# RWKV-7 followed by a quick-GELU MLP: the layout of the MLP weights in DRAM, and the size of the packets in which they arrive

## Chip, core and metric

The kernel runs on one core of a Trainium2 chip. The metric is the device time in microseconds of one execution. All times below are from five executions of the kernel before, one of which was taken by the hardware profiler.

## The reference

A linear-attention block (RWKV-7) with batch 4, 8 heads, 768 steps and head size 40 feeds an MLP of 3072 tokens, model width 320 and hidden width 2048. Cut to what matters:

```python
for t in range(S):                                   # per batch and head, state is 40 x 40
    y[t] = r[t] @ state
    Sa = state @ a[t]
    state = state * w[t][None, :] - outer(Sa, b[t]) + outer(v[t], k[t])
x = y.transpose(0, 2, 1, 3).reshape(B * S, H * D)    # 3072 x 320
h = x @ w_in                                         # w_in 320 x 2048
out = (h * sigmoid(1.702 * h)) @ w_out               # w_out 2048 x 320
```

The attention inputs come as float32. `w_in` and `w_out` come as float64; the kernel reads them as 64-bit integers and makes float32 of them on the chip.

## The kernel before, in words

**Units.** The 768 steps are cut into 12 chunks of 64. A unit is one chunk of one pair of batches with all 8 heads, so there are 24 units, and the state goes from unit i to unit i + 2. For a unit the kernel takes logarithms and sums of the decay, scales a, k and b by them (L583, L585, L588: `ak` and `b` times the decay), forms small score matrices (`ps_N`, `ps_A`, `ps_RV`), inverts a triangular 64 x 64 matrix per head in five levels (`ps_level`, each with copies by ScalarE and transposes by VectorE: L747, L686), solves with it (`ps_B`, `ps_Q`, `ps_T`, `ps_X`) and reads out (`ps_y`). The result goes through DRAM (`x_dram`, L917) and comes back transposed (`xT_all`, L921). Two units, one chunk, make 256 tokens, for which the MLP runs: `ps_up` (x times `w_in`), the activation (L942) and `ps_down` (times `w_out`), then a store. All matrix work is float32 in 64 x 64 tiles of TensorE. All matmuls and weight loads of TensorE go through one helper and so stand on line 275.

**Order of the work.** The code adds tasks to a plan (class `Plan`), each with a rank, costs per engine, what it reads and what it writes. `Plan.order` plays the tasks through a model of the engines, including a model of how TensorE's instructions are brought in blocks of 256 (`BLOCK`, `FETCH`, `BESIDE`, L65, L123 to L143), and so fixes one order for each engine. The instructions are then issued in that order; nothing is reordered while the kernel runs. All loads and stores are issued from SyncE (SP), onto one DMA queue. At most eight of these DMAs are under way: an issue waits until the DMA issued eight before it has landed, and for the last readers of the buffer that it fills.

**Loads.** A unit loads `time`, `RV`, `logw` and from the fifth unit `wc` with 128 rows each, and `ak`, `b` and `rv` in two halves of 40 rows each (L475, L464). Rows are of 1280 to 4096 bytes.

**Weights.** `w_in` and `w_out` are brought in four pieces each, eight in all (`weight(n, ...)`, L406 to L447, n from 0 to 7). A piece is 128 rows, one for each partition, of 1280 doubles, that is 10240 bytes a row and 1.31 MB a piece. One DMA on SP (L442) brings it to a place for raw doubles: a buffer `extra` with two places "a" and "b", two places in `w_sb` that are not in use yet, and one in `xT_all`; the list is

```python
    raws = ["a", "w4", "w6", "b", "x", "a", "b", "a"]
```

Then ScalarE reads the high words (L422), and VectorE makes the exponent, the fraction and their sum in five passes (L426, L430, L431, L434, L438), the last of which writes the float32 weights to `w_sb`. The ranks of the pieces (`RANKS`, L244) place the first five within the first three units' work. The order of elements within a partition's 10240 bytes is that in which `ps_up` and `ps_down` read them.

On the host, `kernel` (L1009) lays the arrays out; `pieces` (L1059) makes an array of shape (4, 128, 1280) of 64-bit integers from each weight matrix, one piece after the other, a partition's 1280 in a row.

Of the kernel before, what the change touches and what calls it, by code (L numbers as in the profile page):

```python
# [225 lines left out]
def rwkv7_gelu_quick(ctx: ExitStack, tc: tile.TileContext, time_d, v_d, w_d, wc_d, ak_d, b_d, rv_d, w_in, w_out, out):  # L226
    nc = tc.nc
# [2 lines left out]
    C = 64  # L230
    MID = C // 2
    NU = time_d.shape[0]
    PIECE = w_in.shape[2]
    NF = w_in.shape[0] * PIECE // DM
    NM = NF // 2
    NK = DM // 64
# [18 lines left out]
    plan = Plan(dict(logw=3, wc=3, G=1, wch=3, wz=2, time=2, ak=2, b=2, rv=2, FT=3, GT=1, kh=2, bh=2, zr=2, rz=2,  # L255
                     A=1, B=1, RV=2, E0=2, W0=2, P21=2, PT=2, W=2, E=2, ES=2, EX=2, T=2, Tc=1, QT=1, zraw=2, zT=1, M=2, x=1, xT=3, g=4, ob=1), 4)
    tiles, psums, drams = {}, {}, {}

    def single(name, shape):
        return const.tile(shape, FP32, tag=name, name=name)  # L260
# [27 lines left out]
    def act(n):  # L288
        return {"ACT": 210.0 + 0.76 * n}
# [105 lines left out]

    extra = single("extra", [128, 4 * PIECE])
    xT_all = single("xT_all", [128, plan.slots["xT"], 2 * NK * 128])
# [8 lines left out]
    def weight(n, rank, src):  # L406
        at = raws[n]
        def raw():
            if at == "x":
                return xT_all[:, 1:].rearrange("p s n -> p (s n)").bitcast(INT64)  # L410
            tile, k = spots[at]
            return tile[:, k * PIECE:(k + 2) * PIECE].bitcast(INT64)

        scale = lambda: w_sb[:, n * PIECE:(n + 1) * PIECE].bitcast(INT32)

        before = [("weight", m) for m in range(n) if raws[m] == at]
        there = [("weight", m) for m in range(n) if raws[m] in (f"w{n}", f"w{n - 1}")]
        word = lambda dt, w: raw().bitcast(dt).rearrange("p (n two) -> p n two", two=2)[:, :, w]

        def rebased(t):  # L420

            nc.scalar.activation(scale().bitcast(FP32), word(FP32, 1), ACT.Prelu, scale=2.0 ** -112, alpha=2.0 ** 32)  # L422

        def bounded(t):

            nc.vector.tensor_scalar(scale().bitcast(FP32), scale().bitcast(FP32), least, most, ALU.max, ALU.min)  # L426

        def exponent(t):

            nc.vector.tensor_scalar(word(INT32, 1), scale(), 3, -2 ** 23, ALU.logical_shift_left, ALU.bitwise_and)  # L430
            nc.vector.tensor_single_scalar(scale(), scale(), 3, op=ALU.logical_shift_left)  # L431

        def fraction(t):
            nc.vector.scalar_tensor_tensor(word(FP32, 1), in0=word(UINT32, 0), scalar=2.0 ** -52, in1=word(FP32, 1),  # L434
                                           op0=ALU.mult, op1=ALU.mult)

        def joined(t):
            nc.vector.tensor_add(scale().bitcast(FP32), scale().bitcast(FP32), word(FP32, 1))  # L438

        one, two = 170.0 + 0.48 * PIECE, 150.0 + 1.05 * PIECE  # L440
        T = lambda *names: [(name, n) for name in names]
        plan.add(rank, {"SP": 350.0}, lambda t: nc.sync.dma_start(raw(), src), reads=before, writes=T("wt"), size=128 * PIECE * 8)  # L442
        plan.add(rank, act(PIECE), rebased, reads=T("wt") + there, writes=T("rebased"))
        plan.add(rank, {"DVE": one, "sbuf": True}, bounded, reads=T("rebased"), writes=T("bounded"))
        plan.add(rank, {"DVE": 2 * one, "sbuf": True}, exponent, reads=T("bounded"), writes=T("exponent"))
        plan.add(rank, {"DVE": two, "sbuf": True}, fraction, reads=T("exponent"), writes=T("fraction"))
        plan.add(rank, {"DVE": two, "sbuf": True}, joined, reads=T("fraction"), writes=T("weight"))  # L447

    def weights():
        for n in range(len(raws)):  # L450
            weight(n, RANKS[n], w_in[n] if n < NQ else w_out[n - NQ])
# [636 lines left out]
```

## Time and profile before

| | us |
|---|---|
| five executions | 719.08, 721.26, 723.46, 723.84, 726.84 |
| median | 723.46 |
| the profiled execution: its own time | 723.84 |
| its span, from first to last instruction | 722.1 |
| TensorE matmuls busy (PE) | 675.4 (94%) |
| TensorE weight loads busy (PEld, beside PE) | 568.0 (79%) |
| VectorE busy (DVE) | 428.3 (59%) |
| ScalarE busy (ACT) | 356.7 (49%) |
| GpSimd busy (POOL) | 189.2 (26%) |
| DMA queue q1, all loads and stores | 67.03 MB, 30.9% of 16 engines |

A profile has a page with busy times, a picture of the span in 40 slices (each digit is a tenth of busy time, or of the full clock for PEclk), the DMA packets, and a chain: the work that ended last, followed back from the end, at each step to what released it. "Issue" in it is time in which an engine waited for nothing that the profile shows. Queries of the trace give busy times in chosen stretches, the chain piece by piece, and a timeline in which the idle time before an instruction stands in brackets with what ended it. The trace also holds a record of each DMA packet (queue, size, start and duration) and of each step of a semaphore.

### The profile page before, as it was taken

To read this page: it belongs to the slowest core of one execution; us is meant where nothing else is said; L and a number is where in the kernel's file an instruction comes from. 1 tells how busy PE (TensorE), PEld (TensorE's weight loads), DVE (VectorE), ACT (ScalarE), POOL (GpSimd) and SP (SyncE) were. 2 spreads that over 40 slices of the span, in tenths; PEclk is the share of its full clock that TensorE was granted. 3 is DMA by queue.
4 is the path that set the end of the run, shared out by engine and by line. 5 is a ranking of instruction groups with operands and counts; after the bars stand their busy time and mean duration, and the time that the engine had idled before them with its cause. 6 is when DMAs were issued, how large, how long until landed. Compare 5 with 4: busy or idle time off the path is not lost.

```text
span 722.1 us, 43527 instructions
## 1 busy us (share of the span) xinstructions
PE 675.4 (94%) x20256; PEld 568.0 (79%) x20256; DVE 428.3 (59%) x739; ACT 356.7 (49%) x705; POOL 189.2 (26%) x260
## 2 busy tenths in 40 slices
PE   4576896999999999999999999999999999999997
PEld 3565785799788789987788789887889988887564
DVE  6669878856767556666756655755656566431000
ACT  4465645456564554555465455457456446342020
POOL 8004323422331431330340320431530320200000
PEclk9869998999999999999999999999999999999999
DMA  7963441432341441351440341431430230111000
GB/s 218 355 253 103 163 152 59 120 97 72 118 115 45 118 117 44 96 152 31 119 137 22 107 141 31 119 104 55 119 110 27 77 104 5 40 49 31 20 3 20
DMA packets 31861, 69.82 MB, mean 97 GB/s; under 512 B 5056, under 2 KB 14272, under 8 KB 30656
## 3 DMA queue, kind: packets, MB, share of 16 engines
q1 hardware_dynamic: 31680, 67.03, 30.9%
q8 instruction: 159, 2.61, 1.5%
q14 instruction: 22, 0.18, 0.1%
HBM read 59.15 MB, written 7.86 MB: 93 GB/s over the span
## 4 chain that ended last, share of the span: by engine, by line
PE 85%; DVE 5%; ACT 3%; DMA 3%; issue 3%; POOL 1%; SPq 0%; POOLq 0%; DVEq 0%; ACTq 0%
PE ps_down L275 28%; PE ps_up L275 27%; PE ps_level L275 8%; PE ps_y L275 5%; PE ps_B L275 4%; PE ps_X L275 2%; PE ps_Q L275 2%; PE ps_T L275 1%; PE ps_N L275 1%; PE ps_rz L275 1%; PE ps_A L275 1%; PE ps_zT L275 1%; PE ps_RV L275 1%; DMA extra<-in_w_in 1%; PE ps_cum L275 1%
## 5 line engine op out<-in xcount | busy, mean ns | idle before, releaser
L275 PE MATMUL ps_up<-xT_all,w_sb 64*64 64x256 f32 x3840 | 249.7, 378 | 2.1 <-ACT g L942 1.5
L275 PE MATMUL ps_down<-w_sb,g 64*64 64x320 f32 x3072 | 246.0, 434 | 3.5 <-DVE w_sb L438 2.5
L275 PEld LDWEIGHTS ps_up<-xT_all,w_sb 64*64 64x64 f32 x3840 | 161.4, 133 | 25.8 <-ACT g L942 1.8
L275 PEld LDWEIGHTS ps_down<-w_sb,g 64*64 64x64 f32 x3072 | 135.7, 134 | 48.3 <-issue 5.1
L670 ACT ACTIVATE EX<-ES,quads 128x256 f32<-128x256 f32 x116 | 52.6, 501 | 49.7 <-DVE ES L665 49.5
L591 POOL TENSOR_TENSOR kh<-time,G 128x320 f32<-128x320 f32 x24 | 21.4, 894 | 185.0 <-PE ps_y L275 89.2
L942 ACT ACTIVATE g<-ps_up 128x1024 f32<-128x1024 f32 x48 | 49.1, 1022 | 39.7 <-PE ps_up L275 39.5
L275 PEld LDWEIGHTS ps_level<-W,EX 64*64 64x64 f32 x2560 | 56.5, 134 | 8.8 <-ACT EX L670 1.7
L716 DVE TENSOR_TENSOR E<-two,ps_level 128x256 f32<-128x256 f32 x80 | 33.2, 415 | 40.5 <-ACT W L714 39.7
L275 PE MATMUL ps_level<-W,EX 64*64 64x64 f32 (+1 forms) x2560 | 55.3, 218 | 1.1 <-POOL EX L672 0.6
L714 ACT COPY W<-ps_level 128x512 f32<-128x512 f32 x51 | 29.9, 585 | 42.8 <-PE ps_level L275 42.6
L275 PE MATMUL ps_level<-PT,EX 64*64 64x64 f32 (+2 forms) x1280 | 35.2, 244 | 13.0 <-DVE EX L686 7.3
L968 DVE TENSOR_TENSOR ob<-ob,ps_down 128x320 f32<-128x320 f32 x24 | 11.6, 485 | 59.2 <-ACT ob L966 58.8
L275 PEld LDWEIGHTS ps_level<-PT,EX 64*64 64x64 f32 x1280 | 32.7, 145 | 17.0 <-issue 7.1
L907 POOL TENSOR_TENSOR x<-zr,FT 128x128 f32<-128x128 f32 x84 | 43.4, 546 | 10.0 <-DVE EX L686 9.8
L583 POOL TENSOR_TENSOR ak<-ak,FT 128x512 f32<-128x512 f32 x21 | 28.1, 1340 | 54.9 <-DMA ak<-in_ak 27.5
L845 ACT COPY B<-ps_B 128x416 f32<-128x416 f32 x36 | 18.2, 506 | 43.4 <-PE ps_B L275 43.1
L275 PE MATMUL ps_y<-RV,kh 64*64 64x104 f32 x768 | 36.1, 250 | 2.2 <-DVE M L861 2.2
L275 PE MATMUL ps_y<-M,bh 64*64 64x104 f32 x768 | 36.4, 249 | 1.8 <-issue 1.8
L665 DVE STREAM_TRANSPOSE ES<-E 128x256 f32<-128x256 f32 x80 | 35.6, 445 | 3.9
L861 DVE TENSOR_TENSOR M<-ps_X,later 128x832 f32<-128x832 f32 x24 | 24.5, 1021 | 18.8 <-PE ps_X L275 18.8
L275 PEld LDWEIGHTS ps_y<-RV,kh 64*64 64x64 f32 x768 | 29.9, 133 | 5.6 <-DVE M L861 2.4
(140 smaller groups left out, 1130.6 us busy)
## 6 DMA issues: line engine op xcount, KB each, us to landing
ak<-in_ak SPq DMA_DIRECT2D x48, 160.0 KB
time<-in_time SPq DMA_DIRECT2D x24, 320.0 KB
rv<-in_rv SPq DMA_DIRECT2D x48, 160.0 KB
xT_all<-x_dram SPq DMA_DIRECT2D x48, 160.0 KB
wc<-in_wc SPq DMA_DIRECT2D x20, 264.0 KB
logw<-in_w SPq DMA_DIRECT2D x24, 160.0 KB
b<-in_b SPq DMA_DIRECT2D x48, 80.0 KB
RV<-in_v SPq DMA_DIRECT2D x24, 160.0 KB
```

Source lines behind the costliest of these rows:

```text
L275: nc.tensor.matmul(o, lhsT, rhs, start=start, stop=True, skip_group_check=True)
L583: plan.add(R, {"DVE": 690.0, "POOL": 1270.0, "sbuf": True}, lambda t: of(t.engine).tensor_mul(ahT(), ahT(), FT_of(i)), reads=T("ak", "FT") ...
L591: plan.add(R + 4, {"POOL": 870.0, "DVE": 490.0, "sbuf": True}, lambda t, n=n, dst=dst: of(t.engine).tensor_mul(dst(i)[:, :, :D], by_head(t ...
L665: plan.add(rank, dve(256), lambda t: nc.vector.transpose(ES(n), source(t)), writes=[key("ES", n, 6)], **reads)
L670: nc.scalar.activation(dst[:, :, h], ES(n), ACT.Copy, scale=quads[:, h, :1])
L714: plan.add(rank, any2(512), lambda t: copy(t.engine)(tiles_of(W(n + 1)), blocks(psum(t, ""), 64)), writes=[key("W", n + 1, 5)], pair=pair)
L716: plan.add(rank, dve(256), lambda t: nc.vector.tensor_sub(tiles_of(E(n + 1)), every(two32, [128, 2, 4, 32]), blocks(psum(t, ""), 64)[:, :, ...
L845: plan.add(R, any2(416), lambda t: copy(t.engine)(dst(), psum(t, "")[:, :, :208]), writes=[("Bv", i)] if x and c > 0 else T("B"), pair=(na ...
L861: plan.add(R + 1, dve(832), lambda t: nc.vector.tensor_tensor(M_of(i).rearrange("p (j b) n -> p b j n", b=2), psum(t, "")[:, :, :416].rear ...
L907: of(t.engine).tensor_mul(x[:, b ^ u, b], both(i)[:, at, :64], FT_of(i)[:, at])
L942: plan.add(-45, act(1024), lambda t: nc.scalar.activation(g_of(c * NQ + q).rearrange("p m r n -> p r m n"), psum(t, "").rearrange("p r (m ...
L968: plan.add(-45, dve(320), lambda t: nc.vector.tensor_add(ob_of(serial), ob_of(serial), psum(t, "")[:, 1, :DM]), reads=[("ob", serial)], wr ...
```

## The change

The host lays each piece out as five blocks of 256 doubles for all 128 partitions, one block after the other: shape (4, 5, 128, 256) in place of (4, 128, 1280). A partition's 10240 bytes of a piece so lie in five runs of 2048 bytes, 262144 bytes apart. The DMA that brings a piece reads the five runs of each partition and puts them side by side in the same place as before. What lies in SBUF afterwards, the plan's costs and ranks, and all other instructions are as before: the order of the instructions on the five engines, and what each waits for, is the same in both programs.

```diff
@@ rwkv7_gelu_quick
-    PIECE = w_in.shape[2]
+    PIECE = w_in.shape[1] * w_in.shape[3]
@@ weight
-        plan.add(rank, {"SP": 350.0}, lambda t: nc.sync.dma_start(raw(), src), reads=before, writes=T("wt"), size=128 * PIECE * 8)
+        plan.add(rank, {"SP": 350.0}, lambda t: nc.sync.dma_start(
+            raw().rearrange("p (g n) -> p g n", g=src.shape[0]), src.rearrange("g p n -> p g n")), reads=before, writes=T("wt"), size=128 * PIECE * 8)
@@ pieces, on the host
         x = x.reshape(4, -1, *x.shape[1:]).transpose(0, 2, 1, 3)
-        return np.ascontiguousarray(x.reshape(4, 128, 1280)).view(np.int64)
+        x = x.reshape(4, 128, 5, -1).transpose(0, 2, 1, 3)
+        return np.ascontiguousarray(x).view(np.int64)
```

## The prediction

> **What bounds the kernel now.** I read the page's top first (busy shares, the slices, the packet counts), then the busy table of the stretch in which weights arrive, then the chain of work there and TensorE's own waits, and last the trace's records of single DMA packets and of semaphores.
>
> The page: TensorE is busy almost without a gap from the ninth slice on; its holes, and the only low digits of its clock, lie in the first fifth, where the DMA row is full.
>
> ```profile
> PE   4576896999999999999999999999999999999997
> ...
> PEclk9869998999999999999999999999999999999999
> DMA  7963441432341441351440341431430230111000
> ...
> DMA packets 31861, 69.82 MB, mean 97 GB/s; under 512 B 5056, under 2 KB 14272, under 8 KB 30656
> ...
> q8 instruction: 159, 2.61, 1.5%
> ```
>
> 31861 - 30656 = 1205 packets are of 8 KB or more. 1024 of these are the weights (8 pieces x 128 rows of 10240 B). The 159 of q8 hold 16384 B each, 256 instructions of 64 B: 159 x 256 = 40704, against the 40512 instructions of PE and PEld. So q8 brings TensorE its own instructions, one block of 256 at a time, on the same 16 DMA engines.
>
> The busy table by stretch (columns: time, PE, PEld, DVE, ACT, POOL, granted clock, DMA share, GB/s):
>
> ```profile
> 13.00:24.80 11.80, 7.84 (x319) 6.41 (x312) 9.12 (x14) 5.27 (x14) 4.14 (x4) 1.00 0.98 353
> 24.80:28.30 3.50, 0.05 (x5) 0.04 (x4) 0.95 (x2) 1.86 (x10) 0.20 (x1) 0.70 0.98 311
> 28.30:36.40 8.10, 6.34 (x168) 5.62 (x171) 6.39 (x8) 2.86 (x4) 1.13 (x1) 0.71 1.00 332
> 36.40:50.00 13.60, 9.87 (x271) 9.21 (x265) 9.43 (x13) 8.93 (x17) 0.14 (x1) 0.50 0.86 312
> 130.00:722.00 592.00, 582.25 (x17276) 487.28 (x17268) 326.73 (x607) 286.26 (x556) 145.90 (x182) 1.00 0.27 78
> ```
>
> From 13 to 50 us the DMA engines are full, and in 24.8 to 28.3 no compute engine is. After 130 us TensorE is 98% busy: a lead won early is kept, as its order of work is fixed. The chain of work and TensorE's timeline (in brackets: idle before, and what ended it) say what that hole is:
>
> ```profile
> 14.29 8.55 DMA extra<-in_w_in
> 22.84 0.02 issue
> 22.86 1.42 ACT w_sb L422
> ...
> 24.80 3.45 issue
> 28.26 1.70 PE ps_level L275 x32
> ...
> 34.28 1.31 issue
> 35.59 0.71 PE ps_level L275 x22
> ```
>
> ```profile
> 21.48 0.34 PE L275 MATMUL ps_A<-ak 64*64 64x64 f32 x6 [1.67 <-issue]
> 28.26 1.08 PE L275 MATMUL ps_level<-PT,EX 64*64 64x96 f32 x20 [3.45 <-issue]
> 35.59 0.37 PE L275 MATMUL ps_level<-PT,EX 64*64 64x32 f32 x12 [1.31 <-issue]
> 52.64 0.25 PE L275 MATMUL ps_y<-M,bh 64*64 64x104 f32 x1 [0.77 <-issue]
> ```
>
> "Issue" means no wait that the profile shows. The packet records name it: q8's packets end at 20.10, 26.98, 34.30 and 51.32 us, and TensorE starts again 1.38, 1.28, 1.29 and 1.32 us later. These are waits for instructions. A block is asked for when TensorE enters the block before it, so its wait can be read: packet start less that entry. Packets of q1 that passed on one engine meanwhile are counted beside it.
>
> | fetch asked at, us | DMA traffic | waited, us | packets passed |
> |---|---|---|---|
> | 15.33, 21.48, 28.26, 35.58, 48.42, 79.91 | 55 to 85% weights | 3.70, 4.37, 4.86, 2.81, 1.91, 3.54 | 19.2, 13.6, 22.2, 20.6, 7.6, 11.9 |
> | 195.9, 208.0, 464.8, 514.3 | small packets, 89 to 96% busy | 1.53, 2.58, 1.62, 1.26 | 13.3, 14.8, 15.9, 12.9 |
> | 75 fetches | under 10% busy | mean 0.56 | 0 |
>
> The second row holds the four longest of the twelve fetches past 100 us with over 80% busy; all twelve waited 1.05 us on average. The count that passes is alike (means 15.9 and 14.2), the time is not. A fetch seems to stand behind some 15 packets, whatever their size.
>
> **The change, part by part.** No instruction moves on any engine, and the waits of all five stand as before; only the eight weight DMAs differ, 640 runs of 2048 B for 128 of 10240 B.
>
> *Packets.* The count grows by 8 x 512 = 4096. A 10240-B packet took 388 ns (median of 1024), a 2048-B packet 84 ns (median of 3840). One engine's share of a piece goes from 8 x 388 = 3.10 to 40 x 84 = 3.36 us: +0.26 us a piece. Ends: 40 x 81 (the shortest record) = 3.24 against the old mean 8 x 444 = 3.55 gives -0.3; the mean rate of 1280-B packets (78.6 ns, 61 ns per KB) makes 126 ns of 2048 B, 5.03 us, +1.5. I take +0.26, from rows of just this size. Nearly all of it is covered. By the semaphore records the pieces landed at 22.84, 26.78, 31.14, 37.89, 43.79, 51.93, 84.11 and 110.86 us; ScalarE's L422 read them at 22.86, 32.43, 37.73, 44.76, 57.41, 60.62, 91.38 and 112.40. Only the first has no slack: 0.25 us on the path.
>
> *Issue on SP.* A weight DMA held SP's queue 0.33 to 0.39 us. No DMA with five runs in a row of the tile is in the trace: 0.33 as now, or 5 x 0.33 = 1.7 us. I take 0.33, since rows of 40 and of 128 runs cost the same. Behind it on SP wait the next loads, but in this stretch a DMA lands 4.7 to 14.5 us after its issue, behind others; that backlog covers either end. Without it, 1.3 us for each of eight.
>
> *Fetches.* With 2048-B packets, 15.9 x 84 = 1.3 us; the four small-packet fetches waited 1.75 on average. I take 1.7; ends 0.6 (idle DMA) and 4.9 (no change). Add 1.1 us for the packet and 1.3 to the restart: 4.1 us from asking to running, where three of these took 6.2, 6.8 and 7.3.
> - Fetch of 15.33: there at 19.4, TensorE ran dry at 19.81. Its 1.67 us go, but ScalarE stands behind the first piece until 22.84, so nothing is won on the path.
> - Fetch of 21.48, now asked at 19.8: there at 23.9, needed at about 25.05 (24.80 + 0.25). The 3.45 go whole.
> - Half clock follows that hole: the 1.70 at 28.26 would be 0.87 + 0.43 = 1.3, as the same two groups took at 22.56 and 23.23: 0.4.
> - Fetch of 28.26: asked at 25.05, there at 29.2, needed 5 to 6 us after asking. The 1.31 go.
> - Fetch of 48.42: TensorE used its block in 3.45 us; 0.6 to 1.2 + 1.0 + 1.3 makes 2.9 to 3.5. Of 0.77 I take 0.65.
> - Fetch of 79.91: wait 3.54 to 1.7; its stall of 0.42 at 85.38 goes.
>
> *What is late next.* Led by 5 us, unit 2's ak meets its landing: 34.76 + 3 x 0.26 = 35.5, then POOL's 1.27, against ps_N at 43.49 - 5 = 38.5: enough, but not for much over 6. The sixth piece lands near 53.4 and is wanted at 60.62 - 5.5 = 55.1: enough.
>
> Sum: +0.25 - 3.45 - 0.4 - 1.31 - 0.65 - 0.42 = -6.0 us. The profiled execution took 723.84 us (span 722.1): 717.8. It stands 0.4 above the median of five, so I say 717.5.
>
> **Two rules weighed.** The Trainium skill's "DMA: Bandwidth & Descriptors", section "Queues, rings and completion order", has each DMA engine drain a whole packet of some 9 to 17 descriptors, at most 64, from one ring before it turns to another. This trace's 13 to 22 records fit; 17 x 84 gives 1.4 us and the sum above, but a turn as long as a DMA's 40 runs on one engine would be 3.4 us and leave the stalls as they are. The same page's "Latency and other measured facts" speaks against the change: rows 512 KiB apart in DRAM moved at 207 GB/s. A partition's runs will lie 256 KiB apart; by an estimate from that page a piece would take 1.31 MB / 207 GB/s = 6.3 us. No row here shows it.
>
> **Rivals.**
> 1. *Fetches wait by bytes or by whole DMAs, not by packets.* For: the long waits are also those with the longest backlog in bytes. Against: 89 to 96% busy small-packet stretches let a fetch in after 1.3 to 2.6 us. Then only the 0.25 us stays: 724.
> 2. *The clock stays up too.* It was 0.50 from 36.4 to 50, after holes of 1.31 and 3.04 us. With the first gone, the 9.3 us of TensorE work on the chain between 40.7 and 51 could take about 5 (ps_X 0.94 for 1.66, ps_Q 0.45 for 0.80). The landings above, and the 3.04-us hole, which waits for ScalarE and stays, leave some 3 us of it: 714.5.
> 3. *Slower: the pieces come too slowly.* The first six are one queue, so each one's delay adds up. The sixth is read at 60.62; for +7.2 us it must land at 67.8, 15.9 late, 2.65 a piece: 6.2 us a piece, or 155 ns a packet. Below that the lead is only eaten. For: stretched records exist (a mean of 126 ns at the 1280-B rate, a longest of 595). Against: the median of 84. At 160 ns: 732.
>
> **How the numbers follow.** Main case 0.50 (714.5 to 721, 717.5 likeliest), rival 1 0.25 (722 to 727), rival 2 0.15 (712 to 716), rival 3 0.10 (over 728). The range 713.5 to 726.5 leaves out rival 3 and the outer ends of 1 and 2. About 1%, 7.2 us, is what a measurement tells from no change. Below 716.2 lie rival 2 and a third of the main case: faster 0.30; slower 0.10; within 0.60.
>
> **What would show it.** Right: 35957 packets; no PE idle of over 1 us to "issue" before 60 us; q8 waits near 1.7 us in 13 to 50; ps_level x32 of 28.26 by 25.5; first L422 near 23.1. Wrong: the 3.45 still there (rival 1); 2048-B packets well over 84 ns and L422 waiting at the fourth to sixth piece (rival 3); a clock of 1.00 in 36 to 50 (rival 2); or a lead at 60 us that is gone by 130, where DVE is 85% busy and could give it back.

## The result, and the profile after

| | before | after |
|---|---|---|
| median, us | 723.46 (89 executions, 717.85 to 728.82) | 726.68 (47 executions, 720.89 to 731.23) |
| ratio, 95% interval | | 1.0047 (1.0035 to 1.0059) |
| the profiled execution, us (span) | 723.84 (722.1) | 724.83 (723.0) |
| DMA packets | 31861 | 35957 |

The changed kernel is 3.2 us slower; the interval of the ratio makes it 2.5 to 4.3. The forecast of 717.5 us is missed by 9 us. The direction is that of rival 1, the size more than the rival's 0.25 us.

The page of the kernel after, the same rows as before:

```profile
PE   4676897999999999999999999999999999999997
...
PEclk9759998999999999999999999999999999999999
DMA  7973542332341331351350351431340230111000
...
DMA packets 35957, 69.82 MB, mean 97 GB/s; under 512 B 5056, under 2 KB 14272, under 8 KB 35776
...
q8 instruction: 159, 2.61, 1.5%
```

The change does what it says: 4096 packets more, none of over 8 KB among the weights, the same bytes. TensorE is again busy from the ninth slice on. Its busy table by stretch, with the columns as before:

```profile
13.00:24.80 11.80, 7.44 (x231) 6.85 (x228) 6.55 (x10) 2.95 (x11) 4.47 (x5) 0.86 0.99 336
24.80:28.30 3.50, 3.50 (x108) 3.50 (x99) 2.63 (x4) 2.32 (x3) 0.00 (x0) 0.54 1.03 323
28.30:36.40 8.10, 3.72 (x132) 2.99 (x128) 5.78 (x8) 4.67 (x13) 0.81 (x2) 0.92 1.02 332
36.40:50.00 13.60, 9.47 (x243) 8.79 (x247) 9.10 (x14) 8.01 (x15) 1.18 (x1) 0.50 0.91 308
130.00:722.00 592.00, 582.53 (x17324) 476.98 (x17312) 329.00 (x611) 286.98 (x557) 146.18 (x182) 1.00 0.27 78
```

In the first stretch TensorE runs 231 matmuls where it ran 319: its first hole, which ended at 21.48 us, now ends at 24.24, and what that held up runs in the second stretch, at a clock of 0.54. The second hole has moved behind it, to 28.46. After 130 us TensorE's matmuls are busy as before (582.53 us, 582.25 before). The rate of the loads is the same within 5% in all four early stretches. TensorE's timeline and ScalarE's show the holes (in brackets: idle before, and what ended it):

```profile
24.24 0.34 PE L275 MATMUL ps_A<-ak 64*64 64x64 f32 x6 [2.31 <-issue]
30.31 0.64 PE L275 MATMUL ps_level<-PT,EX 64*64 64x96 f32 x20 [1.85 <-issue]
37.10 0.63 PE L275 MATMUL ps_level<-PT,EX 64*64 64x32 f32 x13 [1.33 <-issue]
```

```profile
25.14 0.37 ACT L657 COPY P<-ps_N 128x256 f32<-128x256 f32 x1 [2.87 <-PE ps_N L275]
25.41 1.39 ACT L422 ACTIVATE w_sb<-extra 128x1280 f32<-128x1280 f32 x1
```

All three holes are there, 2.31, 1.85 and 1.33 us for 1.67, 3.45 and 1.31. The first is now itself on the chain of work, which before passed it by and went through the first piece's landing:

```profile
21.93 2.31 issue
24.24 0.34 PE ps_A L275 x4
```

ScalarE's L422 is late by it too: the first piece landed at 23.02, but its L422 ran at 25.41 (22.86 before), because ScalarE first copies `P` from `ps_N`, and `ps_N` stood behind the hole.

The table of fetches, made from the packet records as in the prediction (asked when TensorE enters the block before; packets of q1 that passed on one engine):

| kernel | asked at, us | waited, us | packets passed |
|---|---|---|---|
| before | 15.33, 21.48, 28.26, 35.58 | 3.70, 4.37, 4.86, 2.81 | 19, 14, 22, 21 |
| after | 15.67, 24.24, 30.31, 37.10 | 6.19, 3.73, 4.28, 3.26 | 67, 35, 38, 39 |

The forecast had 1.7 us. The four waits are 4.37 us in the mean, 3.94 before, and 1.7 to 3.5 times as many packets pass in them.

### The profile page after: what moved, and what is told of

Same layout as the page of the kernel before. It is cut to its first block, busy times and chain, and to the rows that moved or that the text cites. A ratio compares the mean times of both kernels' runs of the same rounds, so it can differ in the third digit from the quotient of the medians.

```text
span 723.0 us, 43527 instructions
## 1 busy us (share of the span) xinstructions
PE 676.6 (94%) x20256; PEld 560.2 (77%) x20256; DVE 428.5 (59%) x739; ACT 356.8 (49%) x705; POOL 190.6 (26%) x260
## 2 busy tenths in 40 slices
DMA packets 35957, 69.82 MB, mean 97 GB/s; under 512 B 5056, under 2 KB 14272, under 8 KB 35776
## 3 DMA queue, kind: packets, MB, share of 16 engines
q8 instruction: 159, 2.61, 1.5%
## 4 chain that ended last, share of the span: by engine, by line
PE 83%; DVE 6%; DMA 3%; ACT 3%; issue 3%; POOL 1%; SPq 1%; POOLq 0%; DVEq 0%; ACTq 0%
PE ps_down L275 28%; PE ps_up L275 26%; PE ps_level L275 8%; PE ps_y L275 4%; PE ps_B L275 4%; PE ps_X L275 2%; DMA ak<-in_ak 2%; PE ps_Q L275 2%; PE ps_T L275 1%; PE ps_rz L275 1%; PE ps_N L275 1%; PE ps_A L275 1%; PE ps_RV L275 1%; PE ps_zT L275 1%; DMA rv<-in_rv 1%
## 5 line engine op out<-in xcount | busy, mean ns | idle before, releaser
L275 PE MATMUL ps_up<-xT_all,w_sb 64*64 64x256 f32 x3840 | 247.0, 378 | 2.8 <-ACT g L943 1.5
L275 PE MATMUL ps_down<-w_sb,g 64*64 64x320 f32 x3072 | 243.2, 434 | 3.3 <-DVE w_sb L438 2.6
L275 PEld LDWEIGHTS ps_up<-xT_all,w_sb 64*64 64x64 f32 x3840 | 157.4, 133 | 28.3 <-ACT g L943 1.8
L275 PEld LDWEIGHTS ps_down<-w_sb,g 64*64 64x64 f32 x3072 | 129.1, 134 | 52.1 <-issue 4.4
L758 ACT COPY Tc<-ps_level 64x128 f32<-64x128 f32 x80 | 20.7, 259 | 26.6 <-PE ps_level L275 25.7
```

The source lines that it names most:

```text
L275: nc.tensor.matmul(o, lhsT, rhs, start=start, stop=True, skip_group_check=True)
L758: copy(t.engine)(at(Tc_t, i)[HALF[r], 128 * h:128 * h + 128], psum(t, "")[HALF[h], r, :128])
```

## The experiments

In the expectations "turn" and "line" are two forms of rival 1: a block of instructions waits for one whole DMA's share of an engine, or for all that stands in the engine in front of it. "Place" is the pitch of 256 KiB in DRAM. All eight pieces are changed unless it is said otherwise. Ratios are to the kernel before on the same chip, with 95% intervals; the kernel before took 725.87 us beside runs10_1k, pad_2k, split5_2k and split4_10k, 725.13 beside stride4_10k, split10_1k, last4_2k and pool_queue, 724.93 beside only_first_2k, first_10k, after_beside and split5_rows, and 722.42 beside paced_10k, split2_rows and before_again. "Mean wait" is that of the second to fourth fetch (asked at about 21 to 39 us) in the one profiled execution, 4.01 us before and 3.76 after.

### Size of packets, one DMA a piece

**runs10_1k**: the changed kernel with ten runs of 1024 B.

```diff
-        x = x.reshape(4, 128, 5, -1).transpose(0, 2, 1, 3)
+        x = x.reshape(4, 128, 10, -1).transpose(0, 2, 1, 3)
```

> Ten runs of 1024 B for each partition in place of five of 2048 B. If the loss of the change comes from each packet's own cost or from SP held up by many descriptors: +3.2 us for 32 more packets an engine and piece, so 72 more give +7, near 730.5 us. If it comes from what stands in line in front of the instruction blocks: 80 packets of about 45 ns make 3.6 us for 3.36, waits grow by 0.3 us each, 727 to 728 us.

Measured: 729.72 us, 1.0056 (1.0027 to 1.0085). Mean wait 3.80 us; 52 to 64 packets passed. A 1024-B packet took 48 ns (median). So packets of 10240, 2048 and 1024 B let a fetch in after about the same time, with 19, 37 and 58 packets in front of it. It is not a count.

**pad_2k**: the changed kernel with 264 doubles (2112 B) from one run of a partition to the next in place of 262144 B, so that the pitch is no power of two.

```diff
+        x = np.pad(x.reshape(4, 128, 5, 256), ((0, 0), (0, 0), (0, 0), (0, 8)))
...
+            raw().rearrange("p (g n) -> p g n", g=5), src[:, :, :256]), ...
```

> Packets of 2048 B with one DMA a piece as changed, but in DRAM a partition's five runs lie close together, 2112 B apart (a pad of 64 B), in place of 262144 B. Theory 'place': near 723.5 us as before. Theories 'turn' and 'line': as changed, 726 to 727.5 us, waits of 3.3 to 6 us.

Measured: 728.3 us, 1.0029 (1.0003 to 1.0055). Mean wait 3.93 us. Without the pitch a loss remains, of 0.2 to 4 us by this interval, and a 2048-B packet takes 84 ns (median) in both kernels. So the pitch is not needed for the loss; that it has no part in it is not shown.

### Number of DMAs a piece

**split5_2k**: the changed layout, five DMAs of 128 x 2048 B for one.

```diff
-            raw().rearrange("p (g n) -> p g n", g=src.shape[0]), src.rearrange("g p n -> p g n")), ...
+        ... lambda t: [nc.sync.dma_start(raw()[:, 256 * g:256 * g + 256], src[g]) for g in range(5)], ...
```

> The changed layout, but each piece is brought by five DMAs of 128 x 2048 B in place of one DMA with 640 runs; packets stay at 2048 B, one engine's share of a DMA falls from 40 packets (3.36 us) to 8 (0.67 us). Theory 'turn' (an instruction block waits until the DMA in progress has ended on its engine): waits of the blocks asked for in 13 to 50 us fall from 3.3 to 6.2 us to 1.5 us or less, the holes by issue go, and the time is near 717 us. Theory 'line' (it waits for the time of all that stands handed over on its engine, whatever the DMA): eight DMAs under way hold less, but the line is still some microseconds: waits 2 to 4 us, 721 to 725 us. Theory 'place' (runs 256 KiB apart in DRAM are slow): near 726.7 as changed.

Measured: 723.07 us, 0.9957 (0.9935 to 0.9979). Mean wait 2.61 us. It is faster than both kernels.

**split10_1k**: the same with ten DMAs of 1024-B runs.

> Ten DMAs a piece, each of 128 runs of 1024 B; one engine's share of a DMA is 8 x 48 ns = 0.38 us, and SP needs about 10 x 0.33 = 3.3 us to issue a piece, about what it takes to move. Theory 'line': with at most eight DMAs under way the line is at most 3 us and mostly half of it: waits of 1 to 2.5 us, holes of 2 us or less in all before 60 us, ratio 0.990 to 0.996. Against it, SP's issue time may hold the pieces back: the first would land by 1 us later, and then the ratio is 0.996 to 1.002.

Measured: 724.11 us, 0.9993 (0.9970 to 1.0015). Mean wait 1.23 us. Its timeline shows no idle time of TensorE put down to "issue" between 12 and 95 us: what the forecast wanted of the change is here, and nothing is won. (The profiled execution took 727.73 us, 3.6 more than the median of this kernel.) The stretch from 13 to 50 us of this kernel, then of the kernel before:

```profile
13.00:50.00 37.00, 24.23 (x746) 21.58 (x742) 25.74 (x34) 19.08 (x43) 5.75 (x6) 0.71 0.80 240
```

```profile
13.00:50.00 37.00, 24.10 (x746) 21.28 (x742) 25.89 (x35) 18.92 (x43) 5.61 (x6) 0.72 0.94 329
```

The same 746 matmuls in the same time, but the loads move at 240 GB/s for 329. GpSimd's timeline and TensorE's in this kernel name the new wait:

```profile
41.92 1.41 POOL L584 TENSOR_TENSOR ak<-ak,FT 128x512 f32<-128x512 f32 x1 [15.01 <-DMA ak<-in_ak]
```

```profile
33.59 1.56 PE L275 MATMUL ps_level<-PT,EX 64*64 64x96 f32 x32 [2.78 <-DVE EX L687]
40.53 1.56 PE L275 MATMUL ps_level<-PT,EX 64*64 64x96 f32 x32 [4.95 <-DVE EX L687]
```

SP spends some 0.4 us on each of ten issues, and unit 2's `ak`, two DMAs, is issued behind them by 36.7 us (27.1 before) and lands at 41.4; GpSimd takes it up at 41.92. Before, the same step was

```profile
35.27 1.27 POOL L583 TENSOR_TENSOR ak<-ak,FT 128x512 f32<-128x512 f32 x1 [8.79 <-DVE extra L434]
```

In split10_1k VectorE's and TensorE's work waits behind this step.

**split4_10k** and **stride4_10k**: the kernel before with four DMAs of 32 rows of 10240 B, neighbouring rows in the one, every fourth row in the other.

```diff
-lambda t: nc.sync.dma_start(raw(), src)
+lambda t: [nc.sync.dma_start(raw()[32 * g:32 * g + 32], src[32 * g:32 * g + 32]) for g in range(4)]
...
+lambda t: [nc.sync.dma_start(raw()[g::4], src[g::4]) for g in range(4)]
```

> The layout before (packets of 10240 B), but each piece is brought by four DMAs of 32 rows: one engine's share of a DMA falls from 8 packets (3.10 us) to 2 (0.78 us). Theory 'turn': waits of 1.5 us or less, near 717 us, the same as with five DMAs of small packets, since packet size does not matter. Theory 'line': the same as there too, 721 to 725 us. If packet size matters once the DMA is small: this one is slower than the five DMAs of 2048-B packets by over 2 us.

> As the four DMAs of 10240-B packets before, but each takes every fourth row, so that it spreads over all partitions (the 32 neighbouring rows of the last try took 774 ns a packet for 388, which spoiled it). One engine's share of a DMA is 2 packets, 0.78 us, near that of the five DMAs of 2048-B packets (0.67). Theory 'line', in time of what stands ahead, whatever its packets: waits of 1.6 to 3.9 us in 13 to 50 as with those five, and 721 to 725 us where before takes 725.9 (ratio 0.994 to 0.998). If packets of 10240 B hold a block up more than those of 2048 at the same size of DMA: no gain over before, waits of 2.8 to 4.9.

Measured: split4_10k 744.16 us, 1.0255 (1.0215 to 1.0295). It can't be compared on the fetches (10.26 us for the first, 1.59 in the mean of the next three), since its 10240-B packets took 774 ns for 388 (medians): 32 neighbouring rows arrive at half the rate. stride4_10k 724.5 us, 0.9995 (0.9973 to 1.0016), mean wait 2.03 us. Its shorter waits bought nothing, since ScalarE's first L422 ran at 31.46 us:

```profile
31.46 1.35 ACT L422 ACTIVATE w_sb<-extra 128x1280 f32<-128x1280 f32 x1 [7.25 <-DMA b<-in_b]
```

The first piece had landed by 22.68. But in this kernel ScalarE's waits ahead of that L422 are for the semaphores of the first three pieces' DMAs (in split5_2k for those of the first piece alone), and the last DMA of the third landed at 31.31. So the run says nothing on what shorter waits are worth.

### Which pieces, and which queue

**last4_2k**: 2048-B runs in one DMA for `w_out`'s four pieces alone. **only_first_2k**: for the first piece alone. **first_10k**: for all but the first. **after_beside**: the changed kernel again, beside the last two. The edit picks the old or the new `dma_start` (and the layout to go with it) by n; for first_10k:

```diff
+        ... nc.sync.dma_start(raw(), src...) if n == 0 else nc.sync.dma_start(
             raw().rearrange("p (g n) -> p g n", g=src.shape[0]), src.rearrange("g p n -> p g n")), ...
```

> Only the four pieces of w_out (the fifth to the eighth) come in packets of 2048 B; the four of w_in come as before. If the change's loss of 0.47% arises in 13 to 40 us, where the first four pieces and the three holes lie: ratio 0.999 to 1.002. If it arises later, or piece by piece: 1.002 to 1.005.

> Of the eight weight pieces only the first comes as 640 runs of 2048 B in one DMA; the other seven come as 128 rows of 10240 B, as in the kernel before. What is open is where the changed kernel's 3.2 us (ratio 1.0047) are made. 'First': at the first piece, where the fetch asked at 15.67 waited 6.19 us (3.70 before), so that TensorE was late for ps_N and ScalarE's first L422 ran at 25.41 in place of 22.86. Then this kernel loses nearly all of it: a first fetch of about 6 us, first L422 at 25 or later, ratio 1.003 to 1.005. 'Every': each of the eight adds its 0.26 us or holds SP up a little. Then one piece of eight is worth 0.4 us: ratio 1.0005, first L422 near 23.1.

> The complement: the first piece comes as 128 rows of 10240 B, the other seven as 640 runs of 2048 B each in one DMA. 'First': the loss is gone, ratio 0.998 to 1.001, first L422 near 22.9, later fetches still waiting 3 to 5 us as in both kernels. 'Every': seven eighths of the loss stay, ratio 1.004.

> The changed kernel itself, unaltered, beside the three others. By its 47 earlier runs: ratio 1.0047 (1.0035 to 1.0059) of the kernel before; the first fetch wait, 6.19 us in its one profiled execution, should again be over 5 us by 'first'. If it comes out near 3.7 with the same loss, the first piece is not where the time is lost.

Measured: last4_2k 726.7 us, 1.0018 (0.9995 to 1.0041); only_first_2k 724.86, 1.0003 (0.9981 to 1.0026); first_10k 726.38, 1.0027 (1.0000 to 1.0054); after_beside 727.46, 1.0035 (1.0007 to 1.0062). In only_first_2k the first fetch did wait 6.47 us and the first L422 ran late:

```profile
25.44 0.37 ACT L658 COPY P<-ps_N 128x256 f32<-128x256 f32 x1 [4.68 <-PE ps_N L275]
25.71 1.40 ACT L422 ACTIVATE w_sb<-extra 128x1280 f32<-128x1280 f32 x1
```

Yet its time hardly moved: "first" had 1.003 or more, and the interval ends at 1.0026. In first_10k, with L422 at 22.64, the ratio is still 1.0027, though its interval reaches down to 1.0000. "First" falls; the intervals of these runs hold what "every" says, but are too wide to show it.

**pool_queue**: the kernel before with the weights issued by GpSimd, on a queue of their own.

```diff
-lambda t: nc.sync.dma_start(raw(), src)
+lambda t: nc.gpsimd.dma_start(raw(), src)
```

> Packets of 10240 B and one DMA a piece as before, but the eight weight DMAs are issued from GpSimd, on a queue of their own; the first five are free to go at about 11 us, so the DMA engines are as full from 11 to 45 us. If the line in which an instruction block waits is that of the DMA engine, over all queues: waits of 3 to 5 us between 13 and 45 us, as before. If each queue has its own line and the engine takes turns between queues: loads and blocks go beside the weights, waits of 1 to 2 us. The time says little, since the pieces compete with the first units' loads from 11 us on: 715 to 735 us.

Measured: 725.15 us, 0.9993 (0.9967 to 1.0019). The first four fetches waited 5.69, 4.00, 4.08 and 1.17 us, the last of them when 0.83 MB stood queued, the others at 2.8 MB and more. A queue of their own for the weights did not shorten the waits.

### Shorter DMAs, or a slower issue

**split5_rows**: the kernel before, its own layout, five DMAs of 2048 B of each row. **paced_10k**: 1276 of a row's 1280 doubles in one DMA and the last four in four DMAs of 8 B a row. **split2_rows**: two DMAs of 5120 B of each row.

```diff
-lambda t: nc.sync.dma_start(raw(), src)
+lambda t: [nc.sync.dma_start(raw()[:, 256 * g:256 * g + 256], src[:, 256 * g:256 * g + 256]) for g in range(5)]
...
+lambda t: [nc.sync.dma_start(raw()[:, at:to], src[:, at:to]) for at, to in [(0, 1276), (1276, 1277), ..., (1279, 1280)]]
...
+lambda t: [nc.sync.dma_start(raw()[:, 640 * g:640 * g + 640], src[:, 640 * g:640 * g + 640]) for g in range(2)]
```

> The kernel before with its own layout in DRAM, but each piece fetched by five DMAs of 256 doubles of each row, that is 2048-B packets whose runs lie 10240 B apart. It asks whether the gain of the five DMAs (ratio 0.9957 with the blocked layout) needs the new layout. 'Line' (an instruction block waits for whole DMAs' shares of an engine, so shorter DMAs shorten it, wherever they lie in DRAM): the same gain, ratio 0.994 to 0.998, fetch waits of 1.6 to 3.9 us in 13 to 50 us. 'Place' (contiguous blocks matter): packets longer than 84 ns in the median and no gain, ratio 1.000 or more.

> The kernel before, where each piece's DMA brings 1276 of a row's 1280 doubles (one run of 10208 B) and four more DMAs bring the last four, 8 B a row each. SP is so held for five issues a piece, as in split5_rows, but 99.7% of a piece stay in one DMA. 'Line' by the size of single DMAs: fetch waits of 13 to 50 us stay at 3 to 6 us, ratio 1.000 to 1.004. 'Pace' (five issues spread the backlog in the engines, and that alone shortens the waits): waits of 1.6 to 3.4 us as in split5_rows, ratio 0.993 to 0.998.

> The kernel before with each piece fetched by two DMAs of 640 doubles of each row, 5120-B packets. 'Line' by the size of single DMAs: waits between those of one DMA (2.8 to 4.9 us in 13 to 40 us) and of five (1.6 to 2.9): 2.2 to 3.5, ratio 0.997. 'Pace': two issues are 1 us of SP, so little is spread: ratio 0.998 to 1.000.

Measured: split5_rows 720.7 us, 0.9950 (0.9921 to 0.9980); paced_10k 719.92, 0.9968 (0.9944 to 0.9993); split2_rows 722.15, 0.9996 (0.9968 to 1.0025). Mean waits 2.43, 1.85 and 2.50 us. split2_rows has waits as "line" had them and a time as "pace" had it: its waits are as short as those of the kernels with five DMAs, and nothing is won. So a shorter mean wait alone, read in one profile, does not make the gain. The gain needs neither the new layout nor small packets: paced_10k brings 99.7% of a piece in rows of 10208 B by one DMA. "Pace" holds, and "line" by the size of single DMAs falls. SP's timeline shows the pace, in paced_10k some 3.5 to 4.8 us for the issues of a piece (first fence) where a piece's one issue took 0.33 before (second fence):

```profile
13.08 3.50 SPq L442 DMA_DIRECT2D extra<-in_w_in  x5
17.45 4.78 SPq L442 DMA_DIRECT2D w_sb<-in_w_in  x5
23.09 4.43 SPq L442 DMA_DIRECT2D w_sb<-in_w_in  x5
```

```profile
14.29 0.33 SPq L442 DMA_DIRECT2D extra<-in_w_in  x1
```

Two things make this pace, and no run separates them. One is SP's own time, 0.34 us an issue in the mean before and 0.44 to 0.57 in the three kernels with five DMAs a piece (first six pieces). The other is the program's rule of at most eight DMAs under way, of which one piece now takes five. Of the 4.78 us of the second piece, 2.70 pass until the first piece lands at 21.41 and makes room; in split5_rows 20 of the first 30 weight issues start within 0.06 us of such a landing, in paced_10k 6.

TensorE's timeline in paced_10k:

```profile
21.62 0.34 PE L275 MATMUL ps_A<-ak 64*64 64x64 f32 x6 [2.15 <-issue]
26.20 0.64 PE L275 MATMUL ps_level<-PT,EX 64*64 64x96 f32 x20 [1.26 <-issue]
45.59 0.48 PE L275 MATMUL ps_B<-RV,A 64*64 64x104 f32 x9 [1.53 <-issue]
49.32 0.30 PE L275 MATMUL ps_y<-M,bh 64*64 64x104 f32 x1 [1.10 <-issue]
```

The 3.45-us hole of before is one of 1.26, the 1.31 at 35.59 is gone, and new ones come at 45.59 and 49.32.

What a slower issue changes can be counted: the backlog, the bytes of all DMAs issued by SP when a fetch is asked for, less the bytes that the packet records show as moved by then. Means of the second to fourth fetch:

| kernel (packets of weights) | backlog, MB | wait, us |
|---|---|---|
| before, before_again (10240 B) | 2.67, 2.18 | 4.01, 3.33 |
| after, after_beside (2048 B) | 2.07, 2.12 | 3.76, 4.14 |
| runs10_1k (1024 B) | 1.70 | 3.80 |
| split2_rows (5120 B) | 1.80 | 2.50 |
| split5_2k, split5_rows (2048 B) | 1.06, 1.12 | 2.61, 2.43 |
| stride4_10k (10240 B) | 1.07 | 2.03 |
| paced_10k (10208 B) | 0.76 | 1.85 |
| split10_1k (1024 B) | 0.36 | 1.23 |

Over these and the four other kernels with all issues on SP (split4_10k with its slow packets left out; only_first_2k, first_10k, last4_2k, pad_2k: 2.09 to 2.44 MB, 3.22 to 3.93 us) the correlation of the two columns is 0.88. Sorted by size of packet they show nothing: 1024 B has both 3.80 and 1.23 us.

The backlog is not the whole of it. By single fetches, not means of three, the correlation is 0.72. And the first fetch, which the table leaves out, goes the other way: it waited 6.19 and 6.12 us in the two profiles of the changed kernel with 1.68 and 1.90 MB queued, 4.75 in before_again with 2.95. During the 6.19 us the queue of loads moved 2.14 MB, more than had stood there, so bytes issued after the fetch was asked for went ahead of it. The second to fourth fetch of before let only 1.2 to 1.6 of 2.4 to 3.0 MB pass. So a fetch neither waits for all that is queued nor for that alone; what decides between it and the loads stays open.

### The spread of single profiles

**before_again**: the kernel before, unaltered, one execution with a profile.

> The kernel before, unaltered, for a second profile. If its first fetch, asked at about 15.3, again waits 3.4 to 4.2 us, the 6.1 to 6.5 us of the kernels whose first piece comes in 2048-B packets are an effect of the change; if it waits 5 us or more, that wait varies between executions by more than the change moves it, and no single profile can carry the 3 us.

Measured: 723.03 us. Its first fetch waited 4.75 us (3.70 in the other profile), and its holes differ as well:

```profile
22.69 0.34 PE L275 MATMUL ps_A<-ak 64*64 64x64 f32 x6 [2.98 <-issue]
29.74 1.07 PE L275 MATMUL ps_level<-PT,EX 64*64 64x96 f32 x20 [3.72 <-issue]
52.09 0.25 PE L275 MATMUL ps_y<-M,bh 64*64 64x104 f32 x1 [1.65 <-issue]
```

It falls between the two cases that were set out. The start of one and the same matmul, later or earlier than in the first profile of before (us):

| at, in before | before_again | after | after_beside | only_first_2k | split5_rows | paced_10k |
|---|---|---|---|---|---|---|
| 21.60 | +1.21 | +2.76 | +2.38 | +2.56 | -0.43 | +0.13 |
| 41.40 | +0.37 | +1.97 | +3.94 | +1.49 | -4.02 | -3.64 |
| 50.91 | -1.44 | +2.11 | +1.64 | +0.68 | -6.15 | -3.66 |
| 59.23 | -0.76 | +1.16 | +1.62 | +0.80 | -2.15 | -2.03 |
| 73.86 | +2.17 | +1.17 | +4.58 | +3.67 | -3.01 | -2.02 |
| 716.90 | -0.89 | +0.90 | +2.85 | +0.73 | -5.16 | -1.21 |

Two executions of the same program differ by 1 to 2 us at such points. That is the size of what is looked for, and only medians of many executions carry it. Nor is a profiled execution a typical one: it took 722.62 us in paced_10k (median 719.92) and 717.30 in split2_rows (median 722.15).

## Why the prediction was wrong, point by point

- **Packets: right.** 35957 packets; a 2048-B packet took 84 ns in the median. The pieces landed at 23.02, 27.33, 32.23, 38.59, 44.09 and 52.58 us, 0.2 to 1.1 later than before.
- **Issue on SP: right in what the others felt, not in what SP did.** A weight's issue held SP 0.38 us, but some 0.8, and one issue behind them 3.09:

```profile
13.59 0.81 SPq L442 DMA_DIRECT2D extra<-in_w_in  x1
...
18.23 0.39 SPq L442 DMA_DIRECT2D w_sb<-in_w_in  x1
18.67 3.09 SPq L465 DMA_DIRECT2D wc<-in_wc  x1
```

  The backlog covered it as said: unit 2's `ak` was issued at 23.10, 22.91 before.
- **Fetches: this step failed.** The prediction had "A fetch seems to stand behind some 15 packets, whatever their size". It rested on the likeness of two means, 15.9 packets among weights and 14.2 in stretches of small packets. With 2048-B packets the second to fourth fetch let 34.7 to 38.9 pass, with 1024-B packets 51.8 to 63.6, and waited as long as before. What goes with the wait is the backlog in bytes, which the change leaves much as it is (2.07 and 2.12 MB for 2.67 and 2.18): eight pieces of 1.31 MB put into the engines by issues of 0.3 to 0.4 us. The small-packet stretches had short waits with DMA engines as busy, but the forecast did not ask how much stood queued there. It was 0.40 to 0.60 MB at the four fetches in the second row of the prediction's table, and 0.83 to 3.00 MB at the six in the first row, so what was held against rival 1 agrees with it. The four terms of the sum that are fetch holes (3.45, 1.31, 0.65, 0.42) and the 0.4 of clock all hung on this step; -6.2 us goes.
- **The 1.67 us "on no path": half right.** The first hole was put down as harmless since ScalarE stands behind the first piece until 22.84. That holds for 1.67 us and not for 2.31 after a fetch that waited 6.19: then `ps_N`, `P` and L422 come 2.5 us late.
- **What is late next: short.** The chain of waits was followed to a lead of 5 us, with SP's issues at their old places. split10_1k shows the same loads as the bound once SP issues later: `ak` at 41.92 us. And split5_rows, which led by 6.15 us at 50.9, keeps 2.15 at 59.2. Between 50 and 65 us its clock was 0.77 (1.00 before), after a hole of 2.24 us that ended at 47.96:

```profile
50.00:65.00 15.00, 11.37 (x369) 10.18 (x373) 12.93 (x19) 8.70 (x19) 3.60 (x7) 0.77 0.56 177
```

  The kernels with five DMAs, with mean waits of 1.9 to 2.6 us, won some 2 to 4 us of the 6 (-2.3 to -3.6 us by their ratios).
- **Rival 1 was the nearest, and too small.** Of its two forms, paced_10k speaks against waits by whole DMAs. It had 0.25 us, for the first piece's later landing. Measured are 2.5 to 4.3. A longer first fetch (6.19 and 6.12 us in two profiles of this kernel) is not it alone, by only_first_2k; the pitch is not needed for it, by pad_2k. Whether it is the sum of eight small delays, SP's held issues, or both stays open: no run moved them apart by more than its interval.
- **Rivals 2 and 3: no.** The clock in 36.4 to 50 us is 0.50 as before (there it fell at 36.45, ahead of the 3.04-us hole, which lay in 37.67 to 40.71 and so did not bring it about); the pieces came at 84 ns a packet, not 155.
- **The two rules.** The row stands first: 34.7 to 67.0 packets of 2048 B and up to 123 of 1024 B passed a fetch. The Trainium skill's "DMA: Bandwidth & Descriptors", section "Queues, rings and completion order", says that an engine drains a whole packet of 9 to 17 descriptors, at most 64, of one ring before it turns. Waits that go with the backlog and not with such a packet are not told by it, and the longest counts here are above its ceiling, if a record is a descriptor. The other rule, in "Latency and other measured facts" of that page, has 207 GB/s at a row pitch of 512 KiB beside 214 as the full rate, so it hardly speaks against the change, as the prediction has it do. At 256 KiB this case shows 84 ns a packet, and padding moved the time by no more than the intervals.

## What to carry over

When a small transfer waits behind large ones, plot its wait against the bytes issued and not yet moved, not against the count of packets in front; here smaller packets moved the count up to threefold, and the mean wait stayed as it was. Then look at how much of the wait the queue leaves unexplained, as at the first fetch here. What shortened the waits was a slower issue of the same bytes, by SP's time for each issue and by the limit of eight DMAs under way: five issues a piece for one gained (0.9950 to 0.9968), while two gained nothing that shows, and ten made the loads themselves late and gave all of it back. Two profiles of one program differed by as much as the effect looked for, so let medians decide, and let the profile only say where to look.

## What the runs showed of the hardware that was not expected

- One issue on SP was held 3.09 us (2.94 in the second profile of the changed kernel, 4.99 for two issues with 1024-B runs, 0.35 for the same `wc` before), with no wait in the program that explains it. It comes after three pieces of 640 runs (two pieces of 1280), so the number of runs not yet moved is a candidate. But an issue was also held 1.98 us at 39.80 in paced_10k, whose DMAs have 128 runs each; the cause stays open.
- 32 neighbouring rows of 10240 B in one DMA took 774 ns a packet, every fourth row 389, all 128 rows 388.
- A queue of its own for the weights did not let the instruction fetches past them: the first three waited 4.00 to 5.69 us, as long as with one queue.
